# Seeding PSUM from ScalarE and widening a product by one column, with a re-dealt instruction order

## The chip, the cores and the metric

The kernel runs on one core of one Trainium2 chip. The metric is the device time of one execution in microseconds (us); of the kernel before there are three timed runs, and their median is the figure to compare with. Each kernel also has one profiled execution, in which the hardware profiler recorded every instruction; its time and its span (first to last instruction) are given beside the timed runs. In the profile PE is TensorE's matmul, PEld its weight load, DVE is VectorE, ACT is ScalarE, POOL is GpSimd and SP is SyncE, whose queue issues most of the DMAs.

## What is computed

Two sequence layers read the same `x` (2048 positions, 512 features) and a gate mixes them. Cut to what matters:

```
g = sigmoid(sum(x * gate_w))                        # one gate per position
# A: diagonal complex state space, 512 states
h[t] = Lam_bar * h[t-1] + x[t] @ B_bar.T
a    = 2 * real(h @ C.T) + x * Dskip
# B: linear attention, 32 heads of 16 features
q, k, v = x @ wqkv, split into heads
phi(z)  = [softmax(z @ w_phi), softmax(-z @ w_phi)]
o = phi(q) (phi(k)^T v) / (phi(q) sum(phi(k)) + 1e-6)
b = o @ wo
out = g * a + (1 - g) * b
```

Inputs and output are bf16.

## The kernel before

**Tiling.** The 2048 positions are regrouped by their residue modulo 8: `x_load` brings `x` in, transposed, so that tile `ti` (128 positions, 16 tiles) holds positions of residue r = ti // 2. The recurrence then runs over 256 steps of 8 positions each: inside a step the eight residues are combined by products, and from step to step by a scan on VectorE.

**Order by hand.** Every step is a small generator named by a token, and the string `ORDER` is the whole schedule: each token runs its generator on to the next `yield`. `@0` to `@7` give the PSUM banks that the piece takes (there are 8, of 128 x 512 f32 each), `:D` sends an evacuation (the copy out of PSUM, `evac`, lines 117 to 121) to VectorE in place of ScalarE, `:A` sends a DMA to ScalarE's queue. The order of tokens is the program order of PE, DVE, ACT and SP, each of which runs its own instructions strictly in that order. `F:n` are n filler products into a bank that nobody reads.

**The steps that the change and the prediction name:**

- `k`, `v`, `q` (lines 473 to 496): for a tile, four products of 128 x 512 (one for each 128 features of `x`) into one bank, then one evacuation; `k` and `q` into `Xq`, `v` into one of eight buffers `vxb`, where each head's 16 columns are followed by a column of ones. The weights of `k` and `q` have `w_phi` folded in (`W`, `f`, `w`).
- `x`, `n`, `e`, `s` (lines 516 to 564; `X`, `N`, `E`, `S` for queries): the feature map of a group of tiles: maximum and minimum by trees on VectorE (tiles `mxk`, `mnk`, or `mxq`, `mnq`), exponentials on ScalarE (`EEk`, `EEq`), sums by a tree (`smk`, `smq`), the reciprocal by logarithm and exponential (`lg`, `rho`) on ScalarE, and a scaling on VectorE. Query groups end in four DMA transposes into `phT`.
- `a` (line 571): for each key tile, eight products of 128 x 68 add phi(k)^T v into two banks (`kvacc`), and four products of 128 x 1 with the gate's weight `gw_b` (line 582) add the tile's gate logit into a spare column of the second bank. `G` (line 677) clamps the sixteen logits to `nge` and makes the gate of them.
- `g` (line 597): residue r's own input to states j, evacuated to `uv[j][:, r]` (r = 7 to `va`, four copies of 64 partitions). `z` (line 622): the scan, which gives the states at residue 7, `H7`.
- `h` (line 660): the states at residue r from those at residue 7 or r - 1: a product with the diagonal `dg` plus `uv`. For the residues in `H_VECTOR` (1, 2, 4, 5, 6) VectorE adds `uv` as it evacuates (line 672); for 0 and 3 a product with the identity puts `uv` into the bank first (line 667), `dg`'s product adds to it, and `evac` copies the sum out.
- `y` (line 711): 8 products of states with C, 4 with Dskip, into a bank that stays open. `o` (line 725): products `pn` of `phT` with `KVm`, then `ld`, `nu`, `rd` on ScalarE and `on` on VectorE, then a transpose to `oT` by DMA (or by PE for four tiles). `t` (line 761): four products of `oT` with `Wo` add to `y`'s bank, the gate scales it to `ot`, and a DMA stores it.
- DMAs in SP's order: `l8` to `l15` load tiles of `x`, `NR` and `NI` the two parts of B (`Bn`, 512 KB each), `R` transposes parts of `Bn`.

Of the kernel before, what the change touches and what calls it, by code (L numbers as in the profile page):

```python
# [25 lines left out]
P4 U P3 P4 P4 i1 i2 U l12 i1 i2 U F:4 k0@2 k0 NI P2 P3 l10 i0 l9 k1@3 k1 x0 i1 i1 i0 i2 k3@4 l14 x0 k2@5 n0 U M i1 k2  # L26
V2@6 v3@1 i2 x0 i0 v0@7 i0:D i0 v2@0 x0 k3 l8 n0 l13 i3 x0 k5@2 k5 i3 k4@3 v0 R0 x1 k6@5 n0 n0 i3 i3:D x1 x1 i2 k4 n0
v1@4 i3 L V2 k7@2 k7 n1 n1 x1 n1 gw x1 n1 R1 v6@7 e0 e0 v1 k6:D v4@6 n1 x2 n2 v7@3 v7 k11@2 v6 s0 x2 s0 e1 n2 s0 v5@5
v5 s0 s0 R2 D k12@4 R3 k10@3 k9@7 v4 k8@5 n2 l15 s0 e1 k13@6 v2 s1 k10 k14@0 s0 k11 C1 Q2 k8 C4 g20@3 s1 x2 k13 a0@25
k14 a0 n2 s1 k12 g20 x2 g00@6 k9 g30@0 s1 s1 s1 x2 n2 s1 v3 g40@4 x3 g01@3 g10@7 n3 R5 g00 a1 a1 x3 g60@1 n3 e2 R4  # L30
g11@6 g10 x3 g01 n3 e2 x3 e2 e2 n3 g11 k15@3 g60 g10 g30 g40 x3 s2 n3 g70@1 k15 g11 s2 x4 s2 s2 n4 g30 Q1 Q3 x4 n4 e3
e3 x4 C5 n4 Q0 x4 g50@7 g50 g50 s2 g21@4 n4 g21 s2 s2 v8@3 e3 e3 s3 g70 g70 g70 z0 s3 z0 g31@6 g31 s3 z0 z0 v11@0
g41@7 a2 C6 a2 g41 z0 z0 v11 g61@4 a2 g61 C7 w0@1 w0 C3 w1@7 w1 g31 a2 w2@0 w2 w3@4 s3 s3 g51@1 g51 g51 z0 R7 z0 x4
g62@7 w3 z0 z0 g71@6 g71 g02@0 v8 n4 s3 J2 g71 g71 z1 g02 z1 h50@1 h50 J2 z1 e4 e4 q1@4 h10@3 g62 g12@6 h10 g22@0 q2@1
# [15 lines left out]
o12:D y15 o10 o12 o12 o11 o13@7 o13 o13@5 o13 o13 t2 y14 y14 o10 o12@7 t7:A t5:A o12:D o14@5 o14:D t3:A y10 o15@7 t9:A  # L50
y10 o15 o15@5 o15:D o15 o13 t12 o15 o14@7 o14 o14 t12:D t12 t11 t11:D o15@5 o15 o13@7 t10 t6:A t11 y15 o13:D t10 t10
t15 t15 t15:A o14 o14@2 t13 o14:D t13 t13 t14 t14 t14:A
# [16 lines left out]
def kernel(  # L69
# [18 lines left out]
    nc = tc.nc  # L88
# [25 lines left out]
    def bank(shape, dtype, name):  # L114
        return ps.tile(shape, dtype, tag=f"t{sel['banks'].pop(0)}", name=name, bufs=1)

    def evac(out_ap, in_ap):
        if sel["eng"] == "act":
            nc.scalar.copy(out=out_ap, in_=in_ap)  # L119
        else:  # L120
            nc.vector.tensor_copy(out=out_ap, in_=in_ap)
# [55 lines left out]
    gw_b = const.tile([P, KT], BF16, name="gw_b")  # L177
# [60 lines left out]
    nc.sync.dma_start(out=Wv[:], in_=B_wqkv[:, 2 * D:3 * D].rearrange("(k p) n -> p k n", p=P))  # L238
# [234 lines left out]
    def tile_mm(pt, ti, W):  # L473
        for kt in range(KT):
            MM(out=pt[:], lhsT=xT[:, kt, ti * P:(ti + 1) * P], rhs=W[:, kt, :], start=(kt == 0), stop=(kt == KT - 1))  # L475
# [95 lines left out]
    def st_a(n):  # L571
        for u in range(KG[n][1]):
            nt = KG[n][0] + u
            ti = nt
            if nt == 0:
                live["acc"] = [bank([P, 512], F32, f"kvacc{b}") for b in range(2)]
            for m in range(NB):
                MM(out=acc(m), lhsT=live["EE", n][:, u, m].rearrange("p s f -> p (s f)"),
                   rhs=vxb[nt % NVX][:, 4 * m:4 * m + 4, :].rearrange("p h e -> p (h e)"),
                   start=(nt == 0 and m % 4 == 0), stop=(nt == NTI - 1), skip_group_check=True)  # L580
            for kt in range(KT):
                MM(out=live["acc"][1][:, 4 * KVW + ti:4 * KVW + ti + 1], lhsT=xT[:, kt, ti * P:(ti + 1) * P],
                   rhs=gw_b[:, kt:kt + 1], start=False, stop=(nt == NTI - 1 and kt == KT - 1), skip_group_check=True)
# [71 lines left out]
    def hs(r, t, cols):  # L655
        if r == 7:
            return H7[:, t, cols.start + ZP:cols.stop + ZP]
        return HM[:, t, (r - 1) // 2, cols] if r % 2 else HE[r // 2][:, t, cols]

    def st_h(r, j):  # L660
        ph = bank([P, 2, NC], F32, "ph")
        add = (r, j) in H_VECTOR
        for h in range(2):
            t = 2 * j + h
            src = hs(r - 1, t, slice(0, NC)) if r in (2, 4, 6) else hs(7, t, slice(-1, NC - 1))
            if not add:
                MM(out=ph[:, h, :], lhsT=ident[:], rhs=uv[j][:, r, h, :], start=(h == 0), stop=False, skip_group_check=True)
            MM(out=ph[:, h, :], lhsT=dg[:, (r + 1) // 2 if r % 2 else 0, t, :], rhs=src, start=(add and h == 0), stop=True, skip_group_check=True)
# [179 lines left out]
```

## Time and profile before

| | us |
|---|---|
| median of 3 runs | 156.07 (155.94 to 157.04) |
| the profiled execution | 156.63 |
| its span, first to last instruction | 154.6 |
| PE / DVE / ACT busy in it | 147.7 / 131.8 / 129.4 |
| evacuations of `v` to `vx`, 16 on ACT | 9.4 busy |
| products with the gate's weight, 64 | 3.8 busy |
| products with the identity in `h`, 16 | 3.9 busy |

The granted PE clock is 1.00 in every stretch of the span. Busy time of PE overstates its work, since a product's end is modelled and overlaps the next one's start; the distance from one start to the next, where nothing waits, is what a product costs its engine. The same holds for ACT and DVE, whose neighbours overlap by about a tenth of a microsecond. The three engines' busy time by stretch, their timelines and the chain of waits are shown with the prediction.

### The profile page before, as it was taken

The numbers are of one execution on the slowest core, as the hardware profiler recorded it, in microseconds if no ns is written. First come the engines' busy times: TensorE is split into PE (matmuls) and PEld (weight loads), VectorE is DVE, ScalarE is ACT, GpSimd is POOL, SyncE is SP. The second block draws the span as 40 slices with busy tenths as digits, with TensorE's granted clock in tenths as the row PEclk, the third lists the DMA queues.
The fourth block names the chain that finished last, engine by engine and source line by source line (L and its number), as shares of the span: only waits on it lengthen the run. The fifth ranks groups of instructions, "written<-read, shape, count | busy, mean of one in ns | idle before, by whom it ended". The sixth has DMA issues, their size and how long they took to land.

```text
span 154.6 us, 3382 instructions
## 1 busy us (share of the span) xinstructions
PE 147.7 (96%) x1254; PEld 95.6 (62%) x1254; DVE 131.8 (85%) x303; ACT 129.4 (84%) x279; POOL 16.1 (10%) x43
## 2 busy tenths in 40 slices
PE   7999999999999999999999999999998999989990
PEld 7844444797789876888755767454454545545540
DVE  3789999999999999999999999999997966423730
ACT  3489999999999999999999996799497998465652
POOL 8239980000000000000000000000000000000000
PEclk9999999999999999999999999999999999999999
DMA  4785998465475849910000006943169689789742
GB/s 120 158 222 87 168 191 170 89 98 107 97 78 105 174 94 168 184 25 6 0 0 4 0 0 136 141 136 68 34 123 143 117 163 197 150 137 200 208 147 94
DMA packets 50848, 17.55 MB, mean 113 GB/s; under 512 B 44176, under 2 KB 50832, under 8 KB 50832
## 3 DMA queue, kind: packets, MB, share of 16 engines
q1 hardware_dynamic: 48544, 15.36, 53.2%
q10 hardware_dynamic: 2128, 1.97, 4.5%
q8 instruction: 10, 0.16, 0.4%
q14 instruction: 6, 0.05, 0.1%
q0 software_dynamic: 160, 0.01, 0.1%
HBM read 2.64 MB, written 2.10 MB: 31 GB/s over the span
## 4 chain that ended last, share of the span: by engine, by line
DVE 47%; PE 32%; DMA 8%; ACT 6%; issue 4%; DVEq 0%; SPq 0%
PE py L717 9%; DVE smk L511 6%; PE pk L475 6%; DMA oT<-on 5%; PE py L765 5%; PE pgq L601 4%; DMA phT<-EEq 3%; DVE Bn L672 3%; DVE EEk L548 3%; DVE w L641 3%; DVE HM L672 3%; DVE H L652 3%; PE spin L812 3%; DVE EEk L527 2%; DVE EEk L521 2%
## 5 line engine op out<-in xcount | busy, mean ns | idle before, releaser
L601 PE MATMUL pgq<-xT,BT 128*128 128x256 bf16 x256 | 31.2, 272 | 0.0
L475 PEld LDWEIGHTS <-xT 128*128 128x128 bf16 x192 | 18.3, 98 | 18.6 <-DMA xT<-in_A_x_dram 0.8
L601 PEld LDWEIGHTS <-BT 128*128 128x128 bf16 x256 | 24.7, 98 | 3.9
L138 ACT ACTIVATE EEk<-EEk 128x1024 bf16<-128x1024 bf16 x20 | 20.6, 1075 | 0.3 <-DVE EEk L527 0.3
L765 PE MATMUL py<-Wo,oT 128*128 128x512 bf16 x64 | 16.1, 379 | 0.9 <-DMA oT<-on 0.9
L119 ACT CAST uv<-pgq 128x512 bf16<-128x512 f32 x28 | 16.3, 604 | 0.3
L475 PE MATMUL pq<-Wq,xT 128*128 128x512 bf16 x64 | 15.8, 379 | 0.0
L475 PE MATMUL pv<-Wv,xT 128*128 128x512 bf16 x64 | 15.6, 379 | 0.0
L475 PE MATMUL pk<-Wk,xT 128*128 128x512 bf16 x64 | 15.0, 379 | 0.3 <-ACT EEk L138 0.3
L138 ACT ACTIVATE ld<-pn 128x16 f32<-128x16 f32 x32 | 6.2, 193 | 7.6 <-PE pn L736 7.4
L138 ACT ACTIVATE EEq<-EEq 128x1024 bf16<-128x1024 bf16 x12 | 11.8, 1061 | 0.3 <-DVE EEq L527 0.3
L590 ACT ACTIVATE phT<-X,dgB 128x512 bf16<-128x512 bf16 x16 | 11.5, 740 | 0.0
L769 ACT ACTIVATE ot<-py,G 128x512 bf16<-128x512 f32 x12 | 8.0, 684 | 3.5 <-PE py L765 3.3
L119 ACT CAST nu<-pn 128x256 bf16<-128x256 f32 x28 | 10.3, 381 | 0.0
L736 PEld LDWEIGHTS <-phT 128*128 128x128 bf16 x128 | 6.7, 98 | 5.3 <-DMA phT<-EEq 1.2
L765 PEld LDWEIGHTS <-oT 128*128 128x128 bf16 x64 | 5.6, 97 | 6.2 <-DMA oT<-on 1.2
L119 ACT CAST vx<-pv 128x512 bf16<-128x512 f32 x16 | 9.4, 600 | 0.0
L548 DVE TENSOR_TENSOR EEk<-EEk,rck 128x4096 bf16<-128x4096 bf16 (+1 forms) x5 | 9.3, 1859 | 0.0
L119 ACT CAST Xq<-pq 128x512 bf16<-128x512 f32 x16 | 9.1, 610 | 0.2
L736 PE MATMUL pn<-KVm,phT 128*128 128x68 bf16 x128 | 8.0, 194 | 0.8 <-DMA phT<-EEq 0.7
L119 ACT CAST Xq<-pk 128x512 bf16<-128x512 f32 x15 | 8.4, 618 | 0.4 <-PE pk L475 0.4
L511 DVE TENSOR_TENSOR smk<-smk 128x512 bf16<-128x512 bf16 (+4 forms) x18 | 8.6, 476 | 0.1
(177 smaller groups left out, 319.6 us busy)
## 6 DMA issues: line engine op xcount, KB each, us to landing
X<-HM SPq DMA_DIRECT2D x8, 256.0 KB, 4.0
out_dram<-ot ACTq DMA_DIRECT2D x11, 128.0 KB, 2.5
out_dram<-ot SPq DMA_DIRECT2D x5, 128.0 KB, 2.5
C2r<-in_B_wqkv_dram ACTq DMA_DIRECT2D x2, 256.0 KB, 3.3
Wv<-in_B_wqkv_dram SPq DMA_DIRECT2D x1, 512.0 KB, 4.0
Bn<-in_A_B_re_dram SPq DMA_DIRECT2D x1, 512.0 KB, 5.5
Bn<-in_A_B_im_dram SPq DMA_DIRECT2D x1, 512.0 KB, 6.7
Wo<-in_B_wo_dram SPq DMA_DIRECT2D x1, 512.0 KB, 4.6
```

The source lines that it names most:

```text
L119: nc.scalar.copy(out=out_ap, in_=in_ap)
L138: ins = nc.scalar.activation(**kw)
L475: MM(out=pt[:], lhsT=xT[:, kt, ti * P:(ti + 1) * P], rhs=W[:, kt, :], start=(kt == 0), stop=(kt == KT - 1))
L511: VT(out=dst, in0=cur[:, :, :, 0:n, :], in1=cur[:, :, :, n:2 * n, :], op=op)
L548: VT(out=E5, in0=E5, in1=rc.to_broadcast([P, L, 2 * NB, Dh, 4]), op=ALU.mult)
L590: nc.scalar.mul(out=t_, in_=x_, mul=c_)
L601: MM(out=pg[:, h, :], lhsT=BT[:, kt, 2 * j + h, :], rhs=xT[:, kt, r * NC:(r + 1) * NC], start=(h == 0 and kt == 0), stop=(r % 2 == 0 and k ...
L672: VT(out=dst, in0=ph[:], in1=uv[j][:, r], op=ALU.add)
L717: MM(out=py[:], lhsT=hs(r, t, slice(a * P, (a + 1) * P)), rhs=C2B[t], start=(t == 0), stop=False)
L736: MM(out=pn[:, 4 * m:4 * m + 4, :].rearrange("p h e -> p (h e)"), lhsT=ph[:, 4 * hf + m, :], rhs=KVm[:, 4 * hf + m, :], start=(m == 0), st ...
L765: MM(out=py[:], lhsT=oT[:, g, :], rhs=Wo[:, g, :], start=False, stop=(g == HG - 1))
L769: nc.scalar.mul(out=ot[:], in_=py[:], mul=G[:, ti:ti + 1])
```

## The change

Three things change in the code, and the whole order with them.

1. In `h`, residues 0 and 3 (`H_SEED`) no longer have a product with the identity: `evac` writes `uv[j][:, r]` into the PSUM bank (the token `h0j` or `h3j` stands once more in the order for it), and `dg`'s product adds onto that.
2. The gate's weight becomes column 513 of V's weight tile (`Wvg`, 514 wide; `gw` writes the column). V's product is made in two halves of 256 and 257 columns, in two banks; two evacuations of 256 columns and one copy of the single column to `gl` follow, all by the tile's engine (the last one always ScalarE). The 64 products of one column in `a` go, and `G` reads `gl`.
3. `HE`, which uses V's weight tile as a store of states, is indexed by one more dimension, since the tile's rows are 514 wide; no instruction comes or goes with it.

```diff
-H_VECTOR = tuple((r, j) for r in (1, 2, 4, 5, 6) for j in range(4))
+H_VECTOR = tuple((r, j) for r in (1, 2, 4, 5, 6,) for j in range(4))
+H_SEED = tuple((r, j) for r in (0, 3,) for j in range(4))
...
-    Wv = const.tile([P, KT, D], BF16, name="Wv")
+    Wvg = const.tile([P, KT, D + 2], BF16, name="Wv")
+    Wv = Wvg[:, :, 0:D]
+    gl = const.tile([P, NTI], F32, name="gl")
...
     def st_gw():
-        nc.vector.tensor_copy(out=gw_b[:], in_=vec[:, 4, :])
+        nc.vector.tensor_copy(out=Wvg[:, :, D], in_=vec[:, 4, :])
         yield
...
     def st_v(ti):
-        pv = bank([P, D], F32, "pv")
-        tile_mm(pv, ti, Wv)
-        yield
-        evac(vxb[ti % NVX][:, :, 0:Dh], pv[:].rearrange("p (h e) -> p h e", e=Dh))
+        hd = D // 2
+        pv = [bank([P, hd + c], F32, "pv") for c in range(2)]
+        for kt in range(KT):
+            for c in range(2):
+                MM(out=pv[c][:], lhsT=xT[:, kt, ti * P:(ti + 1) * P], rhs=Wvg[:, kt, c * hd:(c + 1) * hd + c], start=(kt == 0), stop=(kt == KT - 1))
+        yield
+        for c in range(2):
+            evac(vxb[ti % NVX][:, 16 * c:16 * c + 16, 0:Dh], pv[c][:, 0:hd].rearrange("p (h e) -> p h e", e=Dh))
+        nc.scalar.copy(out=gl[:, ti:ti + 1], in_=pv[1][:, hd:hd + 1])
         yield
...
-            for kt in range(KT):
-                MM(out=live["acc"][1][:, 4 * KVW + ti:4 * KVW + ti + 1], lhsT=xT[:, kt, ti * P:(ti + 1) * P],
-                   rhs=gw_b[:, kt:kt + 1], start=False, stop=(nt == NTI - 1 and kt == KT - 1), skip_group_check=True)
             yield
...
         add = (r, j) in H_VECTOR
+        seed = (r, j) in H_SEED
+        if seed:
+            evac(ph[:], uv[j][:, r])
+            yield
         for h in range(2):
...
-            if not add:
+            if not add and not seed:
                 MM(out=ph[:, h, :], lhsT=ident[:], rhs=uv[j][:, r, h, :], start=(h == 0), stop=False, skip_group_check=True)
...
-        VS(out=nge[:], in0=live["acc"][1][:, 4 * KVW:4 * KVW + NTI], scalar1=-Z_MAX, scalar2=-1.0, op0=ALU.max, op1=ALU.mult)
+        VS(out=nge[:], in0=gl[:], scalar1=-Z_MAX, scalar2=-1.0, op0=ALU.max, op1=ALU.mult)
```

The string `ORDER` is another one from its first line to its last. Its tokens are the same but for the eight more of `h`; their places, their banks and some of their engines differ. Early lines of both, where the prediction looks:

```diff
-B F:28 l11 F:4 W1@0 W0@1 W2@2 W1:D f1@3 W3@4 f1 W0:D f0@5 f0 NR W2:D f2@6 W3:D f3@0 f3 f2:D V@1 V P P P P2 P2 P2 P2 P2
...
-v1@4 i3 L V2 k7@2 k7 n1 n1 x1 n1 gw x1 n1 R1 v6@7 e0 e0 v1 k6:D v4@6 n1 x2 n2 v7@3 v7 k11@2 v6 s0 x2 s0 e1 n2 s0 v5@5
...
+B l12 F:28 W0@0 W0 W1@1 NI W1:D W2@2 W3@3 W3 f1@4 f0@5 W2:D f1:D f0 f2@6 V@0 f3@1 V P F:4 f3 f2:D k1@2 P P2 P2 U P P2
...
+U k6@3 i3 x1 k6 k7@2 k7 n1 x1 n1 F:4 v2@54 x2 k12@0 n2 x2 n2 x2 k11@6 L e0 e0 s0 v7@17 v7 k8@3 k8 v4@21 x2 l10 s0
```

Work that moves between engines with the tokens' marks: from DVE to ACT two evacuations of `W`, one of `k6`, one `nu` of `o7` and one `ot` of `t11`; from ACT to DVE the evacuations of `f1` and `k5`, two `Abs` of `i`, one scaling of `c4`, the `nu` of half of `o8`, `o9`, `o11` and `o15`, and `ot` of `t7` and `t8`.

More of the change, by code (lines that the diff above doesn't have):

```diff
@@ L30 @@
[L30 to L34, printed above, removed]
@@ L50 @@
[L50 to L54 removed]
+B l12 F:28 W0@0 W0 W1@1 NI W1:D W2@2 W3@3 W3 f1@4 f0@5 W2:D f1:D f0 f2@6 V@0 f3@1 V P F:4 f3 f2:D k1@2 P P2 P2 U P P2
+P2 P2 k1 V2@3 V2 U P4 k2@4 P3 P2 P3 l11 k0@5 k3@0 P4 gw P4 i0 i2 i0 k0 v1@61 i3 i2 i0 i0:D i2 i2:D k3 i0 l8 NR U x0 i3
@@ new lines @@
+i3 x0 k4@3 v1 n0 x0 n0 k4 i1 x0 n0 v0@25 i3:D v0 l9 i1 n0 x0 k2 n0 i1 i1:D n1 v3@06 v3 i2 x1 k5@1 n1 k5:D x1 n1 i1 x1
+U k6@3 i3 x1 k6 k7@2 k7 n1 x1 n1 F:4 v2@54 x2 k12@0 n2 x2 n2 x2 k11@6 L e0 e0 s0 v7@17 v7 k8@3 k8 v4@21 x2 l10 s0
+v6@73 n2 k12 s0 v2 s0 k11 M k10@0 D s0 l13 v4 s0 s0 k13@5 e1 e1 k10 k9@4 k9 R0 R1 g40@6 g40 C4 g60@2 s1 g60 v6 R3 n2
+a0@10 a0 s1 s1 k13 x2 R2 g00@4 g00 s1 s1 v5@62 v5 n2 x3 s1 l15 s1 n3 l14 v8@73 v8 g10@5 g10 g01@4 g20@6 Q0 x3 C2 n3 x3
+R5 a1 n3 x3 e2 e2 a1 e2 e2 k14@2 k14 n3 g20 R4 g10 g01 k15@7 x3 g21@3 Q3 k15 s2 g30@2 g21 g61@6 n3 e3 s2 e3 C3 n4 g30
@@ new lines @@
+g30 s2 n4 g11@5 g50@4 g50 s2 x4 n4 s2 s2 g22@7 x4 e3 g50 e3 n4 x4 g70@3 s2 s3 x4 Q2 g11 g70 g70 g70 g41@2 s3 a2 g22 Q1
+C0 g61 g41 a2 g02@4 a2 z0 z0 s3 z0 g11 C1 C5 s3 w2@3 w2 s3 z0 z0 z0 C7 w1@7 a2 g02 w1 g31@6 g31 g31 w3@2 w3 x4 s3 z0
+z0 n4 z0 g12@5 g12 w0@3 w0 z0 g12 g51@4 g51 g51 e4 C6 g62@7 g62 g71@6 J2 g71 s3 h50@2 g71 h50 h10@3 g71 z1 q3@5 J2 z1
+h10 e4 z1 z1 z1 q1@4 e4 z1 g42@7 g42 e4 s4 q1 g32@6 g32 z1 z1 J0 g32 c4:D c2 s4 z1 z1 q2@2 q2 J0 q0@3 q0 q3 g52@7 g52
+h60@4 h60 xA g72@6 g52 nA xA c4 v11@23 c2 nA v11 s4 a3 g72 g72 xA v9@57 s4 v9 nA g72 z2 z2 v10@42 v10 s4 s4 J3 J1
@@ new lines @@
+h11@3 J1 h11 R6 R7 g63@5 g63 g43@7 g43 J3 q6@6 c4 c0 c0 a3 a3 z2 z2 xA z2 z2 a3 c3 xA v12@42 v12 g03@3 c3 z2 z2 nA g03
+z2 q10@5 z2 c5 q6 q10 g23@7 g13@4 g13 g33@2 g23 g13 nA g33 g53@3 eA c0 s4 g33 c3 c2 h51@6 h51 g53 h12@5 h12 eA g73@7
+h52@4 h52 g53 g73 eA eA g73 h61@2 h61 g73 sA q14@3 v14@65 c6 z3 z3 q5@4 v14 sA z3 z3 O q5 v15@27 v15 sA h31@4 v13@65
+v13 q11@2 a4 z3 h20@7 q14 z3 h31 sA z3 h21@6 z3 h21 h20 h30@3 q15@5 h31 z3 z3 a4 a4 a4 Y h32@4 h32 q7@6 sA sA h41@7
+h41 h30 q15 Y h32 c5 q7 h30 c5 q13@5 q11 h42@4 Y h22@6 h53@7 h62@1 Y h22 h62 q8@3 h53 h02@2 h02 h13@0 h13 c1 c1 c1 h02
@@ new lines @@
+q4@6 h33@1 sA h63@7 h63 sA h40@2 h33 c7 sA q9@0 h23@7 h23 h33 h43@1 h43 q4 c7 c7 c6 c6 q12@6 q8 y2@7 y2 y2 sA h03@1
+h42 h03 h40 q9 sA sA h01@3 h00@4 END X1 y0@0 h03 q12 G N1 o0@2 o0 X1 h00 N1 X1 N1 X1 N1 h01 h01 h00 y0 o1@1 o1 o1@6 o1
+o1 o0@2 X1 N1 o0 o0 o0 y5@3 X2 o2@4 o2 o2@1 o2 o2 o1 X2 N2 X2 y5 y9@6 E1 G y9 E1 o0 o3@2 y1@4 E1 E1 o2 X2 N2 q13 y1 y0
+X2 y1 y5 S1 G S1 t0 S1 G o1 o3 o3@1 o3 o2 y3@5 t2 o3 S1 S1 y6@2 y13@1 N2 y6 t2 t0 o3 o3 t1 N2 y4@7 y9 S1 S1 N2 S1 y4
+y4 X3 N3 E2 E2 E2 E2 X3 X3 t1 N3 t2 X3 N3 y3 X3 y3 S1 y6 S1 o4@0 o4 o4@4 o4 o4 t3 t3 o5@0 o5 o5@4 S2 S2 S1 S1 o5 o5 o4
@@ new lines @@
+S2 y13 y13 o4 N3 t1:A S2 o6@5 o6 S2 o5 o6@0 o6 o5 y7@4 y7 y8@5 o6 N3 S2 S2 o6 S2 y8 y8 t4 t4:D o7@0 t5 o6 E3 t6 E3 E3
+E3 S3 o7 S3 o7@7 y7 t5 o7 o7 S2 S2 S2 y11@0 t6 o7 o8@3 o8:D o8@7 S3 o8 S3 o8 o8 y11 S2 t5:A o7 S3 S3 o9@2 o9 o9@7 o9:D
+o9 o8 o9 o9 S3 y10@3 y10 y10 y12@2 S3 o11@7 o11:D S3 y11 t4:A y12 y12 S3 S3 o11@7 o11 o11 t7 t7:D o10@7 o10 t9 t9:D
+o10@7 o11 o10 t8 o12@4 o12:D t8:D o12@7 S3 o12 o12 o11 t8:A y15@6 o12 y15 o13@4 o10 o12@7 o12:D y14@5 o13 o13@4 o10
+o10 t7:A t9:A o13 o13 t12 o14@7 o14:D o14@4 o14:D t12:D o14 y14 t6:A y15 o13 y14 t0:A o15@7 o15:D o15@4 o15 o15 o15
@@ L176 @@
     vec = const.tile([P, 5, KT], F32, name="vec")
-    gw_b = const.tile([P, KT], BF16, name="gw_b")
     KVm = const.tile([P, NB, KVW], BF16, name="KVm")
@@ L208 @@
     Bn = pBC.tile([P, NT2, D], BF16, name="Bn")
-    HE = [w_.rearrange("p k (a c) -> p (k a) c", a=2) for w_ in (Wk2[:], Wv[:], Bn[:, 0:4, :], Bn[:, 4:8, :])]
+    HE = [w_.rearrange("p k (a c) -> p k a c", a=2) for w_ in (Wk2[:], Wv, Bn[:, 0:4, :], Bn[:, 4:8, :])]
     pAC_g = tc.tile_pool(name="pAC", bufs=1)
@@ L237 @@
         x_load(ti)
-    nc.sync.dma_start(out=Wv[:], in_=B_wqkv[:, 2 * D:3 * D].rearrange("(k p) n -> p k n", p=P))
+    nc.sync.dma_start(out=Wv, in_=B_wqkv[:, 2 * D:3 * D].rearrange("(k p) n -> p k n", p=P))
     for ti in range(4, 8):
```

23 lines of the change are left out of this document (3 added, 20 removed).

## The prediction

> **What bounds the kernel now.** First the page's head and the chain of waits that ended last, then busy time in four stretches cut where the work changes kind.
>
> ```profile
> span 154.6 us, 3382 instructions
> ...
> PE 147.7 (96%) x1254; PEld 95.6 (62%) x1254; DVE 131.8 (85%) x303; ACT 129.4 (84%) x279; POOL 16.1 (10%) x43
> ...
> DVE 47%; PE 32%; DMA 8%; ACT 6%; issue 4%; DVEq 0%; SPq 0%
> ```
>
> ```profile
> 10.00:60.00 50.00, 49.69 (x427) 34.07 (x425) 49.70 (x111) 48.98 (x94) 11.29 (x26) 1.00 0.70 127
> 60.00:98.00 38.00, 38.00 (x350) 27.35 (x348) 37.67 (x83) 35.81 (x67) 0.00 (x0) 1.00 0.25 51
> 98.00:118.00 20.00, 19.15 (x132) 9.54 (x131) 19.82 (x44) 16.30 (x38) 0.00 (x0) 1.00 0.55 91
> 118.00:151.00 33.00, 32.12 (x272) 17.71 (x272) 18.41 (x35) 22.90 (x73) 0.00 (x0) 1.00 0.83 169
> ```
>
> The columns are the stretch, its length, then busy time of PE, PEld, DVE, ACT and POOL, the granted clock, DMA's share and GB/s. To 60 us three engines are full at once. To 98 PE and DVE are, ACT has 2.2 us left. To 118 DVE is full, PE nearly. After that PE alone. The chain passes through DVE more than through PE, so a gain on PE alone is worth at most PE's gain and is lost where DVE or ACT are late instead. The span is 154.6 and the profiled execution 156.63, 2.03 around it; the median, 156.07, is 0.56 below that execution. So median = span + 1.47.
>
> Costs are distances from start to start where nothing waits. They are shorter than durations:
>
> ```profile
> 29.25 0.41 PE L578 MATMUL kvacc<-vx,EEk 128*128 128x68 bf16 x8
> 29.50 0.24 PE L582 MATMUL kvacc<-gw_b,xT 128*128 128x1 bf16 x4
> 29.61 4.53 PE L601 MATMUL pgq<-xT,BT 128*128 128x256 bf16 x40
> ...
> 73.71 0.27 PE L667 MATMUL ph<-uv,ident 128*128 128x256 bf16 x1
> 73.82 0.27 PE L668 MATMUL ph<-H,dg 128*128 128x256 bf16 x1
> ...
> 75.90 1.03 PE L475 MATMUL pv<-Wv,xT 128*128 128x512 bf16 x4
> 76.76 0.49 PE L601 MATMUL pgq<-xT,BT 128*128 128x256 bf16 x3
> ```
>
> Columns: start, time from first start to last end, what. Four gate products take 29.61 - 29.50 = 0.11 us of PE, not 0.24, so 0.025 each (medians from the records: 0.025). An identity product takes 0.11 (0.109). Four products of 512 columns take 0.86 (0.216 each).
>
> **The change, part by part.**
>
> PE: 64 gate products leave, 64 x 0.025 = 1.60 us. 16 identity products leave, 16 x 0.109 = 1.74. V's 64 products of 512 columns become 128 of 256 or 257, 128 x 0.109 - 64 x 0.216 = +0.13. Sum -3.2. Nearly all lies where PE is full: up to PE's first `pn` the work falls by 0.8 (95.7 to 94.9; it came at 98.2 us, and steps of other kinds have been moved across that mark), after it by 2.4 (50.1 to 47.7). The weight loads grow by 64 for V's halves and fall by 80; PEld is 62% busy beside PE, so I cost them at nothing. If one showed, it would be a V half short against its load: 128 x 98 ns of loads stand beside 128 x 109 ns of products, which leaves cover.
>
> ACT, V's evacuations. The rows around the case:
>
> ```profile
> 44.86 1.51 ACT L119 CAST va<-pgq 64x256 bf16<-64x256 f32 x4
> 46.40 0.59 ACT L119 CAST uv<-pgq 128x512 bf16<-128x512 f32 x1
> ...
> 98.61 0.18 ACT L138 ACTIVATE ld<-pn 128x16 f32<-128x16 f32 x1 [0.84 <-PE pn L736]
> 98.69 0.37 ACT L119 CAST nu<-pn 128x256 bf16<-128x256 f32 x1
> 98.94 0.20 ACT L138 ACTIVATE ld<-pn 128x16 f32<-128x16 f32 x1
> ```
>
> 512 columns cost 0.477 from start to start; 256 columns cost 0.253 (`nu`, 128 partitions) or 0.381 (`va`, 64 partitions); 16 columns cost 0.076 (`ld`) if something follows at once, 0.193 by its own duration. I take 0.253 and 0.076, since `nu` has the very shape and a strided source: 16 x (2 x 0.253 + 0.076 - 0.477) = +1.7 us. The upper end is 16 x (2 x 0.381 + 0.193 - 0.477) = +7.6; below nothing is excluded, as 512 columns in two parts can't take less than in one at any of these rows.
>
> [...]
>
> ACT, seeds: eight writes of 512 columns from SBUF into PSUM. No row shows that direction. Nearest are PSUM to SBUF, 0.477, and SBUF to SBUF, 0.625 (the scaled copy of line 590). I take 0.477, whose one side is PSUM too: +3.8 us, at most +5.0, at least +2.0 (half the columns, the `nu` row). Each seed stands ahead of its `dg` product, so PE, which had the identity product without a wait, now waits for ACT; behind it on PE stand that step's products and all that follows. By running sums of the intervals along both orders, the startup idle added, seeds fall within 0.6 us of their product's turn.
>
> Banks: a V tile now holds two of the eight until ACT has emptied both, and a seed holds one from its write on. By the same running sums no product waits more than 0.7 us for its bank up to 98 us; I cost it at nothing where ACT keeps up, and where it doesn't it is the rival of ACT below.
>
> Re-dealing of tokens: ACT gains two `W` (+0.96) and loses `f1` (0.48), two `Abs` (0.62), a scaling (0.63), three `nu` net (0.75), one `ot` net (0.58): -2.1. ACT in all: +1.7 + 3.8 - 2.1 = +3.4. DVE: `f1` +0.61, two `Abs` +0.40, the scaling +0.34, three `nu` net +1.02, one `ot` net +0.66, two `W` fewer -0.68: +2.4, of which 1.0 lies ahead of its last scaling of `EEq` (120.9 to 121.9 of work; it began at 132.37) and the rest in the last stage, where DVE is busy 18.4 of 33 us, at no cost.
>
> The mark that shows ACT's part is its first `ld`: 87.4 us of work lay ahead of it at 98.61, so 11.2 idle, 5.6 of that before 10 us. The work becomes 92.6 (+5.2: the halves and seeds, 5.5, and steps moved across the mark), so 5.6 of startup leaves 98.2. It fits, with nothing to spare; that is the cover, and each us beyond it is a us on PE, whose banks ACT empties.
>
> SP's order. The load of one tile (`l11`) now stands behind the first part of `Bn`:
>
> ```profile
> 14.40 0.74 SPq L284 DMA_DIRECT2D Bn<-in_A_B_re_dram  x1
> 15.19 1.30 SPq L229 DMA_TRANSPOSE xT<-in_A_x_dram  x1
> ...
> 23.69 1.41 PEld L475 LDWEIGHTS <-xT 128*128 128x128 bf16 x8 [0.80 <-DMA xT<-in_A_x_dram]
> ```
>
> In the kernel before, the tile in that slot was issued at 15.19 and landed at 20.52, and PE waited 0.8 for a later one. In the new order `k11` comes after 17.1 us of PE work, and PE's idle until there was 2.0: it is due at 19.1. Wait 1.4 us; at most 15.19 + 6.5 (the slowest such landing) - 19.1 = 2.6, at least nothing. I take 1.4. ACT and DVE wait with PE there, as all k work follows.
>
> The clamp of `G` reads SBUF in place of PSUM, once; the copy of `gw` comes before V, and its input landed at 7.37 us, before the first V product: nothing for either.
>
> Sum: span 154.6 - 3.2 + 1.4 = 152.8, median 154.3, profiled execution 154.8.
>
> **The rivals.**
>
> *PE's gain in full*: `l11` lands in time. Span 151.4, median 152.9. For it: landing times vary from 2.8 to 6.5. Against: the neighbour took 5.3.
>
> *DVE's chain* (not slower by much, but no gain): DVE is 99% busy from 60 to 118 us, and its last scaling feeds the last transposes, whose landings (137.9 to 143.2) end 11.4 us before the span does. With 1.0 more ahead of it, span 155.6, median 157.1. Against: DVE idled 5.1 us between 98 and that scaling, waiting for others, and less PE work ahead makes these waits shorter.
>
> *ACT becomes the bound* (slower). V's halves at the `va` row and the one-column copy at its own duration, seeds at 0.625: 5.9 + 1.2 = 7.1 us more than I count. The first `ld` then comes at 105.3 to 105.7, and PE, with 47.7 of work, its 2.5 of idle and the tail of 3.8 behind it, ends the span at 159, median 160.4. It is slower than 157.6 when the first `ld` is more than 4.0 us late, for instance halves at 0.381 alone (32 x 0.128 = 4.1). For: ACT is at 98% up to 60 us. Against: `nu` has the halves' shape. [...]
>
> That the change would not do what it says is excluded by its instruction list: no one-column product and no identity product of line 667 is left, and 32 half evacuations stand in place of 16.
>
> **How the numbers follow.** A measurement of this kernel tells about 1% from no change: below 154.5 is faster, above 157.6 slower. My forecast has 0.50; with the wait between 0 and 2.6 its own range is 152.9 to 155.5, 0.36 of it faster and 0.14 the same. Full gain 0.08, faster. DVE's chain 0.21: 0.15 the same, 0.06 slower (a landing as slow as 4.75 us in place of 3.9 adds 0.85). ACT 0.21: 0.17 slower, 0.04 the same. Faster 0.44, same 0.33, slower 0.23. The range reaches from 152.6, a little below the full gain, to 158.6, about the middle of ACT's case, which leaves some 0.15 out.
>
> **What would show it.** Right if the half evacuations are some 0.25 apart on ACT and the seeds about 0.48; if PE's only new wait near 20 us is a weight load of `xT` for 0 to 2.6 us; if the first `ld` comes before 100; if DVE's last scaling of `EEq` begins by 133 and PE ends 3 us earlier than 150.8, less the wait. Wrong if PE waits for ACT between 20 and 98 us for more than 2 us in sum (ACT's case), or if PE waits for `phT` in the last stage (DVE's case), or if PE's busy sum does not fall by about 3.

## The result and the profile after

| | before | after |
|---|---|---|
| median of 16 runs (us) | 156.41 (155.77 to 157.04) | 157.32 (156.97 to 159.1) |
| ratio, 95% interval | | 1.0066 (1.0048 to 1.0084) |
| span of the profiled execution (us) | 154.6 | 155.3 |

The changed kernel is 0.66% slower, where 154.3 us and a gain were forecast: within 1% of the kernel before and inside the wide range, but outside the forecast's own (152.9 to 155.5) and with the other sign. The page's head and its chain of waits:

```profile
span 155.3 us, 3394 instructions
...
PE 145.3 (94%) x1238; PEld 98.0 (63%) x1238; DVE 134.1 (86%) x309; ACT 132.8 (86%) x313; POOL 15.8 (10%) x43
...
ACT 49%; PE 18%; DMA 10%; SPq 9%; DVE 8%; issue 4%
```

PE's busy time did fall, by 2.4 us. But half of the chain is ACT now, where before it was 6%. Busy time by stretch (columns: stretch, length, then PE, PEld, DVE, ACT, POOL, granted clock, DMA share, GB/s), of the changed kernel:

```profile
10.00:60.00 50.00, 48.86 (x437) 37.23 (x436) 49.13 (x110) 49.00 (x108) 10.43 (x25) 1.00 0.71 130
60.00:85.00 25.00, 24.86 (x226) 19.79 (x225) 24.75 (x54) 24.79 (x59) 0.00 (x0) 1.00 0.28 60
85.00:100.00 15.00, 14.65 (x115) 8.79 (x113) 14.70 (x34) 14.91 (x32) 0.00 (x0) 1.00 0.18 35
```

and of the kernel before, cut at the same times:

```profile
60.00:85.00 25.00, 25.00 (x238) 18.73 (x236) 24.76 (x52) 24.60 (x46) 0.00 (x0) 1.00 0.25 46
85.00:100.00 15.00, 15.00 (x139) 9.80 (x138) 14.91 (x37) 12.48 (x27) 0.00 (x0) 1.00 0.38 68
```

From 85 to 100 us ACT had 2.5 us left and has none now. The waits of PE (column: us in total, times, longest) show a second thing, which the forecast had only as the mark of its rival of DVE's chain:

```profile
PE pn L744 <- DMA phT<-EEq: 1.9, 2, 1.4
...
PE pk L477 <- DMA xT<-in_A_x_dram: 1.1, 1, 1.1
PE py L773 <- DMA oT<-on: 0.7, 1, 0.7
```

The wait for `xT` was forecast (1.4). The wait for `phT` was 0.7 before. The single prices came out as taken. ACT's timeline (start, time from first start to last end, what):

```profile
14.41 0.69 ACT L120 CAST vx<-pv 128x256 bf16<-128x256 f32 x2
14.94 0.22 ACT L495 COPY gl<-pv 128x1 f32<-128x1 f32 x1
14.99 0.66 ACT L120 CAST Xq<-pk 128x512 bf16<-128x512 f32 x1
...
98.91 1.13 ACT L120 CAST ph<-uv 128x512 f32<-128x512 bf16 x2
99.94 0.61 ACT L120 CAST Wk<-ph 128x512 bf16<-128x512 f32 x1
```

Two halves take 14.94 - 14.41 = 0.53 us from start to start (0.506 was taken), the one column 0.05 (0.076), a seed (99.94 - 98.91) / 2 = 0.52 (0.477).

### The profile page after: what moved, and what is told of

It reads as the page before. It is cut to its first block, busy times and chain, and to the rows that moved or that the text cites. A ratio compares the mean times of both kernels' runs of the same rounds, so it can differ in the third digit from the quotient of the medians.

```text
span 155.3 us, 3394 instructions
## 1 busy us (share of the span) xinstructions
PE 145.3 (94%) x1238; PEld 98.0 (63%) x1238; DVE 134.1 (86%) x309; ACT 132.8 (86%) x313; POOL 15.8 (10%) x43
## 4 chain that ended last, share of the span: by engine, by line
ACT 49%; PE 18%; DMA 10%; SPq 9%; DVE 8%; issue 4%
ACT EEk L139 11%; PE py L725 8%; SPq L231 8%; ACT Xq L120 7%; ACT uv L120 7%; DMA phT<-EEq 6%; PE py L773 5%; ACT phT L594 5%; ACT vx L120 4%; DMA xT<-in_A_x_dram 4%; ACT va L120 3%; ACT EEq L139 2%; ACT ph L120 2%; DVE smk L518 2%; PE pn L744 2%
## 5 line engine op out<-in xcount | busy, mean ns | idle before, releaser
L139 ACT ACTIVATE EEk<-EEk 128x1024 bf16<-128x1024 bf16 x20 | 21.1, 1147 | 0.0
L477 PEld LDWEIGHTS <-xT 128*128 128x128 bf16 x128 | 12.1, 97 | 12.1 <-DMA xT<-in_A_x_dram 1.5
L120 ACT CAST uv<-pgq 128x512 bf16<-128x512 f32 x28 | 17.0, 667 | 0.0
L491 PE MATMUL pv<-Wv,xT 128*128 128x256 bf16 (+1 forms) x128 | 16.2, 273 | 0.0
L491 PEld LDWEIGHTS <-xT 128*128 128x128 bf16 x128 | 12.4, 98 | 3.1
L120 ACT CAST vx<-pv 128x256 bf16<-128x256 f32 x32 | 11.1, 432 | 0.4 <-PE pv L491 0.4
L594 ACT ACTIVATE phT<-X,dgB 128x512 bf16<-128x512 bf16 x15 | 10.4, 733 | 0.0
L120 ACT CAST Xq<-pk 128x512 bf16<-128x512 f32 x15 | 9.4, 657 | 0.7 <-PE pk L477 0.7
L744 PE MATMUL pn<-KVm,phT 128*128 128x68 bf16 x128 | 7.5, 195 | 2.3 <-DMA phT<-EEq 1.9
L120 ACT CAST nu<-pn 128x256 bf16<-128x256 f32 x25 | 9.6, 396 | 0.0
L518 DVE TENSOR_TENSOR smk<-smk 128x512 bf16<-128x512 bf16 (+4 forms) x18 | 8.1, 449 | 0.1
```

Of the source, the lines that this page charges most:

```text
L139: ins = nc.scalar.activation(**kw)
L491: MM(out=pv[c][:], lhsT=xT[:, kt, ti * P:(ti + 1) * P], rhs=Wvg[:, kt, c * hd:(c + 1) * hd + c], start=(kt == 0), stop=(kt == KT - 1))
L518: VT(out=dst, in0=cur[:, :, :, 0:n, :], in1=cur[:, :, :, n:2 * n, :], op=op)
L594: nc.scalar.mul(out=t_, in_=x_, mul=c_)
L744: MM(out=pn[:, 4 * m:4 * m + 4, :].rearrange("p h e -> p (h e)"), lhsT=ph[:, 4 * hf + m, :], rhs=KVm[:, 4 * hf + m, :], start=(m == 0), st ...
```

## The experiments

All ratios are to the kernel before, run beside it on the same chip, with 95% intervals; 0.1% is 0.16 us.

### Is any engine free? One load moved, and work added to each engine

`e1_tile_load_first` puts the load of tile 11 back ahead of `NI`:

```diff
-... W1@1 NI W1:D ... P2 P3 l11 k0@5 ...
+... W1@1 l11 NI W1:D ... P2 P3 k0@5 ...
```

> The changed kernel with one move in SP's order: the load of tile 11 stands ahead of the first part of B again. Base is the changed kernel, 157.3 us (before 156.4). Theory 'work of ACT and DVE': in the changed kernel DVE lost 0.1 us and ACT 0.8 while PE waited 1.05 for that tile, so with the wait gone the time falls by 0 to 0.4: 156.9 to 157.3. Rival 'the wait for the tile': all of PE's wait comes back at the end, 156.2 to 156.3. In both the wait of PE for xT near 20 us is gone.

Measured 1.0104 (1.0061 to 1.0146): no gain. The wait did not go, it moved: `k11` no longer waits, but the tiles behind it do (PE waits 0.9 us for `xT` in two places and 0.9 for ACT). The first tile that is issued behind a 512 KB load of B lands 5.6 and 6.0 us after its issue in the changed kernel, 5.4 and 6.5 in this run; tile 11, ahead of both loads here, lands after 2.8.

`e2_pe_more`, `e3_act_more` and `e4_dve_more` repeat work that is there already:

```diff
-        for h in range(2):
+        for h in (0, 1) * (3 if (r, j) in PE_MORE else 1):
```

```diff
             evac(ph[:], uv[j][:, r])
+            if (r, j) in ACT_TWICE:
+                evac(ph[:], uv[j][:, r])
```

```diff
-            VT(out=dst, in0=ph[:], in1=uv[j][:, r], op=ALU.add)
+            for _ in range(2 if (r, j) in DVE_TWICE else 1):
+                VT(out=dst, in0=ph[:], in1=uv[j][:, r], op=ALU.add)
```

> The changed kernel with the two products of six steps of h (residues 5, 6 and 1, j 0 and 1) made three times over, the same result: 24 x 0.109 = 2.6 us more on PE between about 55 and 90 us. Theory 'work of ACT and DVE': PE waits there (its lost time grows from 3.7 at 75 us to 5.0 at 100), so of the 2.6 us about 1.3 fills waits: 158.3 to 158.8. Rival 'PE still sets the time': 159.9.

> The changed kernel with five of the eight seeds written twice: 5 x 0.52 = 2.6 us more on ACT between about 60 and 98 us. Theory 'work of ACT and DVE', with ACT without slack up to its first ld at 100.9 us: 159.3 to 159.9. If DVE alone sets the time and ACT has slack: 157.3 to 158.3.

> The changed kernel with the VectorE sum of four steps of h made twice: 4 x 0.60 = 2.4 us more on DVE between about 55 and 90 us. Theory 'work of ACT and DVE', with DVE without slack up to its last scaling of EEq: 159.3 to 159.7. If ACT or PE alone set the time: 157.3 to 158.3.

| | added | ratio | against the changed kernel (1.0066) |
|---|---|---|---|
| e2, PE | 2.6 us | 1.0153 (1.0102 to 1.0204) | +1.4 us |
| e3, ACT | 2.6 us | 1.0265 (1.0228 to 1.0301) | +3.1 us |
| e4, DVE | 2.4 us | 1.0295 (1.0242 to 1.0348) | +3.6 us |

None of the three has room: ACT and DVE pass on all that they get and more (for ACT the excess lies within the intervals; why DVE passes on more was not settled). PE seemed to have half its room; the last experiments show that e2 also lost a delay that the changed kernel has, and against a kernel without that delay (e17, 0.9999) it pays 2.4 of its 2.6 us.

### The parts undone, one at a time, in the changed order

`e5_no_seed` has the identity products back and no seeds, `e6_no_half` has V in one bank and the gate's products back, `e7_order_only` both.

```diff
-H_SEED = tuple((r, j) for r in (0, 3,) for j in range(4))
+H_SEED = tuple((r, j) for r in () for j in range(4))
```

```diff
-        pv = [bank([P, hd + c], F32, "pv") for c in range(2)]
...
+        pv = bank([P, D], F32, "pv")
+        tile_mm(pv, ti, Wv)
...
+            for kt in range(KT):
+                MM(out=live["acc"][1][:, 4 * KVW + ti:4 * KVW + ti + 1], lhsT=xT[:, kt, ti * P:(ti + 1) * P],
+                   rhs=gw_b[:, kt:kt + 1], start=False, stop=(nt == NTI - 1 and kt == KT - 1), skip_group_check=True)
```

> The changed kernel with its order, but the eight seeds undone: the 16 products with the identity are back in the place of the seeds' products, and ACT writes no seed: ACT -8 x 0.52 = -4.2 us, PE +1.74, DVE as in the changed kernel. Theory 'ACT and DVE are full and PE's gain is spent waiting': ACT has slack again, DVE's work is as before the edit and PE's added work fills its waits between 75 and 100 us (1.3): -0.5 to +0.5 against the changed kernel, 156.8 to 157.8. Rival 'ACT alone sets the time': most of 4.2 us less, limited by PE, 155 to 156. Rival 'PE sets the time': 159.0.

> The changed kernel with its order and its seeds, but V in one bank and one evacuation again and the 64 products with the gate's weight back: ACT -16 x 0.10 = -1.6 us, PE +1.47, most of it before 60 us; DVE the same. Theory 'ACT and DVE are full': -0.5 to +0.5, 156.8 to 157.8. Rival 'the second bank and the two evacuations of V make PE wait': 155.5 to 156.2. Rival 'PE sets the time': 158.8.

> The changed kernel's order with both parts undone, so that every engine's operations are those of the kernel before, but for the steps dealt to other engines: against the changed kernel ACT -5.8 us, PE +3.2, DVE the same. Theory 'ACT and DVE are full': DVE's last scaling of EEq still begins near 134, PE's 145.9 us of work with 3.4 of startup and tile wait and some 2 of late waits end near 151.5, so 157 to 158: the order without the change is no better than with it. Rival 'the change itself costs, the order is good': as fast as the kernel before or faster, 155.5 to 156.4.

| | seeds | V's halves | ratio |
|---|---|---|---|
| changed kernel | yes | yes | 1.0066 (1.0048 to 1.0084) |
| e5 | no | yes | 1.0012 (0.9983 to 1.0042) |
| e6 | yes | no | 1.0185 (1.0148 to 1.0222) |
| e7 | no | no | 1.0112 (1.0078 to 1.0146) |

Read down and across: V's halves with the gate's column gain 1.0% without seeds (e7 to e5) and 1.2% with them; that is 1.6 to 1.9 us for the 1.47 us that they take off PE. The seeds lose 0.5 to 0.7%, though they take 1.74 us off PE. And the order alone loses 1.1%, 1.75 us. None of the expectations held as written. By its ratio e5 comes to 156.6 us, between the theory (from 156.8) and the rival of ACT alone (155 to 156); e6 to 159.3, nearest to the rival 'PE sets the time' (158.8); e7 to 158.2, just above the theory (157 to 158). V's gain is real: the trace of the kernel before has no wait of PE from 25 to 75 us, so what is taken off it there is seen.

### Which seeds, and the tile's load once more

`e9_no_seed_tile_first` is e5 with the load of e1; e10 and e11 keep four of the eight seeds; e12 is e7 with the load of e1.

```diff
-H_SEED = tuple((r, j) for r in () for j in range(4))
+H_SEED = tuple((r, j) for r in (3,) for j in range(4))
```

> The changed kernel without the seeds (identity products back) and with tile 11 loaded ahead of the first part of B; V's halves stay. Theory now: the seeds (4.2 us on ACT, all between 84 and 100 us, where ACT of the kernel before had 2.5 us idle) cost more than PE's 1.74 is worth; V's halves gain their 1.5 us, since PE is full from 25 to 75 us; and the tile's wait costs in full where ACT leaves room. Then this kernel is 0.7 to 1.2 us faster than without the seeds alone (ratio to the kernel before 1.0012): ratio 0.994 to 0.997. Rival 'the tile's wait is hidden in any case, since moving the load alone gave nothing': 1.000 to 1.003.

> As the run without seeds and with tile 11 first, but the four seeds of residue 3 are kept (those of residue 0 are undone): ACT +2.1 us between 84 and 94 us, PE -0.87. Without seeds ACT is busy 11.4 of the 15 us from 85 to 100, so 2.1 us fit. Theory 'what fits costs nothing, and DVE has no slack there': within 0.5 us of the kernel without seeds, either way. Rival 'every seed costs, since PE has to wait for ACT to come round to it': +0.4 to +1.0, half of what the eight cost. Rival 'PE's gain is free': -0.9.

> As the run without seeds and with tile 11 first, but the four seeds of residue 0 are kept (those of residue 3 are undone): ACT +2.1 us, of it 1.6 between 97.9 and 100, just ahead of the first ld. Theory 'ACT carries the late seeds past 100 us and its exponentials of the first query group come later': 0.4 to 1.0 slower than without seeds. If seeds cost only by their sum: the same as with those of residue 3 alone.

> The changed order with both parts undone (ratio 1.0112 to the kernel before) and tile 11 loaded ahead of the first part of B. Theory 'the order's loss is the tile's wait, 1.0 to 1.8 us, and DVE's added 0.8 us': 1.0 to 1.4 us faster than the order alone, ratio 1.002 to 1.005. Rival 'the loss is in other places of the order': ratio 1.009 to 1.012.

Measured 1.0009 (0.9982 to 1.0036), 1.0043 (1.0018 to 1.0068), 1.0075 (1.0050 to 1.0099) and 1.0146 (1.0107 to 1.0184). The load's place gains nothing in any of these kernels: e9 came out as its rival said, e12 slower than either of its two cases (its interval reaches into the rival's). Four seeds seemed to cost about half of what eight do, and those of residue 0 more than those of residue 3, as if ACT's load were the cause. The next pair tests that.

### The seeds' two sides apart

`e13_no_uv` has neither seed nor identity product (uv is left out of the sum for residues 0 and 3); `e14_act_load_only` has the identity products, and ACT's copies go to a dead tile.

```diff
-            evac(ph[:], uv[j][:, r])
+            evac(BD[:].rearrange("p (c a) b -> p c (a b)", c=2), uv[j][:, r])
```

> The changed kernel with neither seeds nor identity products: in residues 0 and 3 of h the residue's own input uv is left out of the sum, so PE has its 1.74 us less and ACT writes nothing for it (V's halves stay). Against the kernel without seeds (ratio 1.0012 to the kernel before). Theory 'PE's gain in h is worth something, since PE is without idle from 85 to 100 us there, and the seeds' cost on ACT eats it': 0.5 to 1.2 us faster than without seeds, ratio 0.993 to 0.998. Rival 'DVE is full, so the products were free to remove and worth nothing': 0.999 to 1.003.

> The changed kernel with the identity products back, and ACT, at the places of the seeds, copying uv to a dead tile in SBUF that nobody reads: PE as in the kernel without seeds, ACT +4 to 5 us between 84 and 100 us, and no product waits for the copies themselves. Theory 'ACT's load alone costs': 0.9 to 2.0 us slower than without seeds, ratio 1.007 to 1.014. Rival 'the wait of the products for their seed costs, the load doesn't': 1.000 to 1.003.

Measured 1.0041 (1.0017 to 1.0064) and 1.0031 (0.9999 to 1.0062). Both went against the theory. ACT's load of eight copies costs 0.3 us over e5 (1.0012), uncertain by 0.7, so it is not told from nothing and is at most about 1 us. And a kernel with 1.74 us less on PE and nothing more on ACT is no faster, if anything slower. So the products' number itself seemed to do harm.

### What comes with fewer products: a load of code among the transposes

The landing times told where. The first query group's four transposes to `phT` (SP's issues: start, time over all four), the first `pn` that wait for them, and what the DMA queues carried meanwhile, in the changed kernel:

```profile
114.93 6.76 SPq L570 DMA_TRANSPOSE phT<-EEq  x4
```

```profile
118.73 1.02 PE L773 MATMUL py<-Wo,oT 128*128 128x512 bf16 x4
121.13 0.43 PE L744 MATMUL pn<-KVm,phT 128*128 128x68 bf16 x8 [1.37 <-DMA phT<-EEq]
```

```profile
q8 instruction: 1, 0.02, 3.0%
issues: line engine op xcount, KB each, median us to landing
phT<-EEq SPq DMA_TRANSPOSE x2, 4.7
```

The last answer is for 116.2 to 120.3 us. One packet of the instruction queue, 16,384 bytes, starts at 117.27 us by the records and takes 1.96; the two transposes in flight land 4.9 and 4.6 us after their issue, where undisturbed ones take 2.7 to 2.8. In e5 and e14, with 16 more products, it starts at 115.3 to 115.5, ahead of the transposes; they land after 2.7 to 3.2, and PE has no wait there. In e13, which lacks the products, it starts at 118.82 and PE waits 1.2 us. The kernel before has it at 115.65, among its own transposes, issued from 113.06 on, which land after 3.1 to 4.8, and waits 0.7. In e10 and e11 it starts at 116.70 and 116.90, also among them, and PE waits 0.4 and 0.7, so the cost of four seeds in these two runs may be the packet's in part. `e17_code_earlier` aims at that packet with 20 tiny products where PE waits for a load anyway (the other packets of the queue move too); `e18_filler_control` spends the same time in 9 larger ones.

```diff
-... n2 x2 n2 x2 k11@6 ...
+... n2 x2 n2 x2 T:20 k11@6 ...
...
+        if tok == "T":
+            for _ in range(int(eng)):
+                MM(out=spin[:, 0:1], lhsT=fillw[:], rhs=fillw[:, 0:1], start=True, stop=True)
+            continue
```

> The changed kernel with 20 filler products of one column (20 x 0.025 = 0.5 us, 40 instructions on PE) just ahead of tile k11, where PE waits 1.05 us for a load in any case. In the trace of the changed kernel a 16 KB transfer of the instruction queue starts at 117.27 us, among the transposes of the first query group (issued 116.21 and 117.57, landed 4.9 and 4.6 us later in place of 2.8), and PE then waits 1.4 us for phT; with the 32 PE instructions of the identity products it starts at 115.32 there, ahead of the transposes (issued from 116.11 on, all landed after 2.8 to 3.2 us), and PE does not wait. Theory 'less PE work moves the loads of PE's code onto the transposes': 40 more instructions bring the transfer to about 113.7 us, ahead of the first transpose, the wait for phT near 121 us goes, and the time falls by 0.5 to 1.1 us: ratio 0.9995 to 1.0035. Rival 'the delay of the transposes is not from the code load, or not on the path': 1.005 to 1.008, as the changed kernel (1.0066).

> The control: in the same place 9 filler products of 128 columns, the same 0.5 us of PE in 18 instructions in place of 40. Theory 'code loads': the transfer comes at about 115.6 us, still among the transposes (the first is issued at 114.9, the second at 116.2), a transpose is still late by some 2 us: ratio 1.005 to 1.009. Rival 'the fillers themselves change something, by their time': as the run with the 20 fillers of one column.

e17: 0.9999 (0.9966 to 1.0032). e18: 1.0057 (1.0030 to 1.0084). The same views of e17, the last for 115.9 to 120 us:

```profile
115.61 5.29 SPq L570 DMA_TRANSPOSE phT<-EEq  x4
```

```profile
119.13 1.02 PE L773 MATMUL py<-Wo,oT 128*128 128x512 bf16 x4
119.99 0.42 PE L744 MATMUL pn<-KVm,phT 128*128 128x68 bf16 x8
```

```profile
q1 hardware_dynamic: 2613, 0.66, 70.8%
issues: line engine op xcount, KB each, median us to landing
phT<-EEq SPq DMA_TRANSPOSE x4, 2.8
```

No instruction packet, all four transposes in 2.8 us, no wait, though they were issued 0.7 us later than in the changed kernel. The packet starts at 114.71 here, and at 116.40 in e18, where the first transpose took 3.55 and SP 2.27 us over it. Forty more instructions of PE brought it 2.6 us forward (the expectation had 113.7), 18 brought it 0.9, so it moves with the number of PE's instructions. That it carries PE's code is the author's reading; no trace shows it directly. In the changed kernel PE ran 262, 265 and 231 products and weight loads between the packets at 68.82, 83.32, 100.56 and 117.27 us, and 323 up to the next, at 138.15. The two transposes in flight there land about 2 us late, beside a packet of 1.96 us; how a packet holds up a transpose is not shown.

Two things speak for this packet and not another. In both e17 and e18 the first `ld` comes at 101.45 us, so what parts them comes later; and their next packet starts at 132.9 and 133.1, nearly level. PE's wait alone does not carry the loss: in e18 it waits only 0.4 us for the first group's `phT`, and yet e18 is as slow as the changed kernel. The delay shows on VectorE, between its first `mxq` and its last scaling of `EEq`. The two ends of that stretch in the changed kernel, then in e5:

```profile
99.14 0.68 DVE L518 TENSOR_TENSOR mxq<-Xq 128x1024 bf16<-128x1024 bf16 x1
134.23 1.22 DVE L566 TENSOR_TENSOR EEq<-EEq,rhoq 128x2048 bf16<-128x2048 bf16 x1
```

```profile
99.92 0.68 DVE L518 TENSOR_TENSOR mxq<-Xq 128x1024 bf16<-128x1024 bf16 x1
133.74 1.22 DVE L566 TENSOR_TENSOR EEq<-EEq,rhoq 128x2048 bf16<-128x2048 bf16 x1
```

That is 35.1 and 33.8 us. Of the changed order's traces, the fifteen with a granted clock above 0.99 fall in two groups. Where the packet starts ahead of the transposes (e2, e5, e7, e9, e12, e14, e17) the stretch takes 33.0 to 34.0 us, median 33.8; where it starts among them (the changed kernel, e1, e6, e8, e10, e11, e13, e18) 34.0 to 35.7, median 34.8. The difference, 1.0 us, is about what e17 gains.

### GpSimd, and the old order

`e8_pool_sums` gives six additions to the idle GpSimd; `e15_before_v_seven` puts V's halves into the order of the kernel before, for seven tiles for which a second bank looked unused; e16 adds two steps of `h` moved from VectorE to ScalarE.

```diff
-        VT(out=out_ap, in0=ta, in1=tb, op=ALU.add)
+        (nc.gpsimd if k in POOL_C else nc.vector).tensor_tensor(out=out_ap, in0=ta, in1=tb, op=ALU.add)
```

```diff
-... v7@3 v7 ... v5@5 v5 ... v11@0 ...
+... v7@34 v7 ... v5@54 v5 ... v11@01 ...
```

```diff
-H_VECTOR = tuple((r, j) for r in (1, 2, 4, 5, 6) for j in range(4))
+H_VECTOR = tuple((r, j) for r in (1, 2, 4, 5, 6) for j in range(4) if (r, j) not in ((4, 1), (6, 3)))
```

> The changed kernel with six of the eight sums that make C (the 128x512 bf16 additions of steps c0 to c5) on GpSimd, which is idle there, in place of VectorE: DVE 6 x 0.335 = -2.0 us between about 60 and 95 us. Theory 'ACT and DVE are full': DVE's first mxq comes earlier by what ACT allows, 0.4 to 1.2 us, and the time is 156.1 to 156.9. If DVE does not set the time: 157.3, unchanged. If GpSimd's additions slow VectorE down beside them or come too late for their readers: 157.5 or more.

> The kernel before, its order and all its steps, with V in two halves and the gate's column for seven tiles (5, 7, 9, 11 to 14), which have a second bank free; the other nine keep the gate's products. PE -7 x 0.092 = -0.64 us, ACT +0.7 +0.3 in G, DVE +0.1. Theory 'DVE is full there too (lost time 6.2 at 25 us, 6.5 at 100), so less PE work is not seen': ratio 0.998 to 1.002. Rival 'PE sets the time of the kernel before': 0.995 to 0.997.

> As the run before it, and two steps of h (residue 4, j 1 and residue 6, j 3), which VectorE ends just ahead of its first mxq, done with identity products and a copy by ScalarE in place of VectorE's sum: DVE -1.2 us, ACT +0.95 between 94 and 98 us, where it idles 2.0, PE +0.44. Theory 'PE and DVE both set the time and ACT has room in this place': 0.4 to 1.0 us faster than the kernel before, ratio 0.9935 to 0.9975. Rival 'ACT is late with the last steps and holds up pn': 1.000 to 1.005.

e8: 1.0258 (1.0226 to 1.0290), slower; what it showed stands in the last section. e15: 1.0687 (1.0655 to 1.0719), e16: 1.0691 (1.0669 to 1.0713). The waits of PE in e15:

```profile
PE pv L494 <- ACT va L120: 2.7, 2, 2.3
PE pv L494 <- DVE HM L688: 2.6, 1, 2.6
PE pv L494 <- ACT vx L120: 1.7, 1, 1.7
```

Each is a V product that waits for its second bank to be emptied by another step. Whether the old order would have had a use for less PE work (the question of e15) stays open: the banks decide first. It shows that the halves do not fit into the old order with these banks; whether another choice of banks would have done was not tried. If the order is counted as their price, its 1.75 us leave nothing of their 1.6 (e5, 1.0012).

## Why the prediction was wrong, point by point

The measured path from the kernel before to the changed one, each step a difference of two measured ratios, beside the forecast. With the intervals taken as independent, the steps are uncertain by 0.5 to 0.7 us each:

| step | measured | forecast |
|---|---|---|
| the order and its re-dealt steps (e7), which also takes the packet off the transposes | +1.75 us | +1.4 |
| V's halves and the gate's column (e7 to e5) | -1.6 | -1.47 |
| seeds for identity products, packet out of the way (e5 to e17) | -0.2, not told from 0 | -1.74 |
| the code packet among the transposes (e17 to the changed kernel) | +1.05 | none |
| sum | +1.0 | -1.8 |

**V's halves** were right in place and size: PE's products, ACT's 0.263 and 0.05, and PE as the bound of that stretch.

**The order** was right in size only. The wait for `xT` came (1.05 us, at 19.5 to 20.5), but that it would go if tile 11 landed in time, the premise of the rival with the full gain, is refuted by e1, e9 and e12. What else is in the 1.75 us was not taken apart. By sums of start-to-start intervals the order has 98.1 us of PE work ahead of the first `pn` in e7 where the kernel before has 95.7; and VectorE has 0.8 us of re-dealt steps ahead of its first `mxq`, an estimate from their prices. The kernel before has a wait of 0.7 us beside its own packet, too, which e7 has not; what that is worth was not measured.

**The step that failed** is the sum over PE, in its term of 1.74 us for the identity products, taken off the span in full because "Nearly all lies where PE is full". The runs show -0.2 us in its place with the packet out of the way (e5 to e17, not told from 0), and +0.8 as the changed kernel stands (e5 to it). The rows held the warning: the products lie from 85 to 100 us, where DVE is as full as PE (14.91 of 15 us before) and where ACT had 2.5 us left for 4.2 us of seeds. The prediction itself says that a gain on PE alone is lost where DVE or ACT are late instead, and then did not apply this to the term.

What swallowed the 1.74 us is not shown. About half of it is still there when VectorE begins its first `mxq`: 99.14 us, against 99.92 in e5 and 99.25 in e13, which has neither seeds nor products. These are single executions, and the wait for `xT` alone differs between them by up to 0.6 us. Whether DVE's own work or ACT's seeds hold back the rest is open: e13 would tell if its packet were moved as in e17, and that was not run.

**The rival of DVE's chain**, at 0.21, had the last scaling of `EEq` 1.0 us later and the median at 157.1. The scaling came 1.9 us later (134.23) and the median is 157.3, but the nearness is in part luck: 1.2 us of the delay are there at the first `mxq`, and the stretch behind it is one that the packet lengthens. Nor is a us at the scaling a us at the end: in e17 it comes at 133.63, 1.3 us later than before, and the time is that of the kernel before. The two lines of the kernel before:

```profile
97.92 0.69 DVE L511 TENSOR_TENSOR mxq<-Xq 128x1024 bf16<-128x1024 bf16 x1
132.37 1.22 DVE L559 TENSOR_TENSOR EEq<-EEq,rhoq 128x2048 bf16<-128x2048 bf16 x1
```

**The cover on ACT** was read over too long a stretch. The 11.2 us that ACT idled ahead of its first `ld` were held against 5.2 us of added work. But all eight seeds fall between 84.7 and 100 us, where ACT had 2.5 us; it is full there now. The first `ld` comes at 100.90 and not by 98.2 plus the tile's wait. Yet the seeds are not the reason for that: without them, in e5, ACT is busy 11.41 of these 15 us and the first `ld` is no earlier. The changed kernel, then e5:

```profile
100.90 0.23 ACT L139 ACTIVATE ld<-pn 128x16 f32<-128x16 f32 x1
```

```profile
101.39 0.18 ACT L139 ACTIVATE ld<-pn 128x16 f32<-128x16 f32 x1
```

It follows the first `pn`, at 100.27 and 101.00 us. That ACT's load is a large cost was the next theory, and e14 limits it: the same copies without the products' dependence gave 1.0031 against 1.0012, intervals that overlap. The rival of ACT as the bound, with halves at 0.38, did not occur.

**What no part of the forecast had** is the code packet, 1.05 us. The forecast counted PE's instructions for their time, not for the place at which their code is loaded.

## What to carry to other kernels

Read slack in the stretch in which the added work lies: cut the windows at the edit, not at the next milestone, and then undo the edit to see whether the missing slack cost anything. When several engines are full, time taken off one of them may be worth nothing, here 1.74 us of PE, and adding a little work to each engine in turn tells which are full. When a kernel's instruction count changes and its DMA landings move with nothing to explain it, look at the instruction queue: a few filler instructions where an engine waits anyway can move a load of code off a transfer on the path (here 40 instructions moved it 2.6 us, and e17 came to 0.9999 from 1.0066).

## What the hardware showed that was not expected

A 16 KB packet of the instruction queue took 0.9 to 2.0 us in the traces of the kernel before and the changed one, and in the changed one a transpose in flight beside it landed 2.2 us later (4.9 in place of 2.7); in this kernel its place was worth 0.6% to 0.7% (e18 and the changed kernel against e17).

GpSimd's additions slowed VectorE down while they ran in e8. Its timeline, GpSimd and then VectorE:

```profile
72.93 3.38 POOL L599 TENSOR_TENSOR C2r<-phT 128x512 bf16<-128x512 bf16 x2 [5.32 <-ACT phT L595]
```

```profile
70.16 0.41 DVE L636 TENSOR_TENSOR ms<-va,T2s 128x512 bf16<-128x512 bf16 x1
...
73.93 1.37 DVE L649 TENSOR_TENSOR mc<-w,T2c 128x512 bf16<-128x512 bf16 x1
75.23 1.37 DVE L652 TENSOR_TENSOR ms<-w,T2s 128x512 bf16<-128x512 bf16 x1
```

A VectorE product of 0.41 us took 1.37 beside these two additions on GpSimd. The second addition ends at 76.31 us (72.93 + 3.38) and VectorE's second product at 76.60 (75.23 + 1.37); what makes VectorE slow is not shown. How much of e8's loss comes from this and how much from sums that are late for their readers was not taken apart.

A write by ScalarE from SBUF into PSUM cost 0.52 us for 512 columns from start to start (the seeds at 98.91 us of the changed kernel), against 0.477 from PSUM to SBUF in the kernel before.
